# A two-layer Mish block on one core: x tiles 2-3 by a plain load and TensorE transposes instead of the DMA transpose, and ScalarE's first load behind a memset

## The chip, the core and the metric

One core of a Trainium2 chip. Its engines are TensorE (matmuls, accumulating into the 8 banks of PSUM), VectorE, ScalarE, GpSimd and SyncE. Data moves between device memory and the on-chip SBUF by 16 DMA engines; a transfer is issued by SyncE or ScalarE here, each with a queue of its own, and raises a semaphore when it has landed. The metric is the time of the program on the device in microseconds. Lower is better.

## The reference

x is 2048 rows of 512, w1 is 512 x 1792, w2 is 1792 x 512, all bf16.

```python
h = jnp.einsum("bsd,df->bsf", x, w1) + b1
sp = jnp.log1p(jnp.exp(-jnp.abs(h))) + jnp.where(h > 0, h, jnp.zeros_like(h))
act = h * jnp.tanh(sp)                      # Mish
return jnp.einsum("bsf,fd->bsd", act, w2)
```

## The kernel before

The rows of x are taken in four blocks of 512 (four tiles j of 128 rows each). For a block the first projection computes h transposed: for each of 14 column tiles f of w1, four matmuls (the k tiles of the contracted 512) accumulate a 128 x 512 piece in one PSUM bank. ScalarE adds the bias and applies Mish in one instruction into a_sb (L170). Then the second projection takes each of the four row tiles: 14 matmuls over f accumulate 128 x 512 outputs, VectorE copies them to o_sb (L181) and SyncE stores them. So a stage is 56 matmuls of the first projection (L164), then 56 of the second (L193), four times over. The order on every engine is the order in which the code is written; each engine waits on semaphores where the code says so.

The first projection needs x transposed (xT: 512 features over partitions). Blocks 1 to 3 get it from a DMA transpose issued by SyncE (`load_xT`). Block 0 is split so that TensorE can start early: x tiles 0-1 come by a plain load in which each partition takes two consecutive rows of x (2 KB), into x_nat; TensorE transposes them in eight 128 x 128 pieces (`transpose_x`, L145, by the identity matrix that GpSimd builds), into PSUM banks 6, 5 and 4, and VectorE copies them to xT (L149). Because each partition takes rows 2p and 2p+1, the columns of xT are the even rows and then the odd rows, and the stores of output tiles 0 and 1 put the rows back by the same pattern. Tiles 2-3 come by a DMA transpose.

Ahead of that, TensorE runs ten dummy matmuls (L133) on a constant. Behind the transposes stand, in this order: 16 matmuls of 256 columns over x tiles 0-1 (k by k, f 0 to 3 within each k), 16 of 256 columns over x tiles 2-3 (f by f, k 0 to 3 within each f), which complete the first four banks, then f 4 to 7 at 512 columns, and the rest.

Weights: w1 for f 0-3 comes in two pieces on ScalarE's queue (k 0-1, then k 2-3, `FIRST`), and behind them b1. On SyncE's queue stand x_nat, the DMA transpose of tiles 2-3, w1 for f 4-7 in two pieces, w1 for f 8-13, w2 in two pieces, and the DMA transposes of blocks 1 to 3. The bias is turned into a column per f by VectorE: a memset of b1_pad (L122), a copy, four 32 x 32 transposes and a cast (L204 to L209); ScalarE's first Mish waits for that.

Of the kernel before, what the change touches and what calls it, by code (L numbers as in the profile page):

```python
# [5 lines left out]
P = 128  # L6
# [26 lines left out]
def bass_standalone__dense_activation_mish__prompt_kernel(  # L33
# [10 lines left out]
    BF, F32 = dt.bfloat16, dt.float32  # L44

    _, S, D = x.shape
    F = w1.shape[1]
    KT, FT = D // P, F // P
    assert (S, D, F) == (2048, 512, 1792) and sum(BLOCKS) == S
    x2, out2 = x[0], out[0]  # L50
# [3 lines left out]
    F0 = 4  # L54

    with ExitStack() as es:
        def sb(name, shape, t):
            return es.enter_context(nc.sbuf_tensor(name, shape, t))

        x_nat = sb("x_nat", [P, 2, D], BF)  # L60
        xT = sb("xT", [P, KT, S], BF)
        w1_sb = sb("w1_sb", [P, KT, F], BF)
        w2_sb = sb("w2_sb", [P, FT, D], BF)
# [1 line left out]
        b1_pad = sb("b1_pad", [32, P], BF)  # L65
# [3 lines left out]
        ident = sb("ident", [P, P], BF)  # L69
# [4 lines left out]
        def sem(name):  # L74
            return es.enter_context(nc.semaphore(name))

        sp = Stream(nc.sync, None)
        pe = Stream(nc.tensor, sem("c_pe"))
        dve = Stream(nc.vector, sem("c_dve"))
        act = Stream(nc.scalar, sem("c_act"))  # L80
        pool = Stream(nc.gpsimd, sem("c_pool"))

        def load(q, dst, src, name, transpose=False):
            s = sem(name)
            (q.eng.dma_start_transpose if transpose else q.eng.dma_start)(dst, src).then_inc(s, 16)  # L85
            return (s, 16)

        t_w1, t_w2, t_xT = {}, {}, {}

        def load_w1(q, ks, a, b):  # L90
            t = load(q, w1_sb[:, ks, a * P:b * P], w1v[:, ks, a * P:b * P], "s_w1_%d_%d" % (ks.start, a))
            for f in range(a, b):
                for k in range(ks.start, ks.stop):
                    t_w1[k, f] = t
# [6 lines left out]
        def load_xT(lo, hi):  # L101
            t = load(sp, xT[:, :, lo:hi], x2[lo:hi, :], "s_xT%d" % lo, True)
            for j in range(lo // P, hi // P):
                t_xT[j] = t

        for ks in FIRST:
            load_w1(act, slice(*ks), 0, F0)

        x01 = x2[0:2 * P, :].rearrange("(p j) d -> p j d", j=2)
        out01 = out2[0:2 * P, :].rearrange("(p j) d -> p j d", j=2)  # L110
        t_xn = load(sp, x_nat[:, :, :], x01, "s_xn")
        t_b1 = load(act, b1_nat[:, :], b1.rearrange("(j p) -> j p", p=P), "s_b1")
        load_xT(2 * P, 4 * P)
        load_w1(sp, slice(0, 2), 4, 8)
        load_w1(sp, slice(2, KT), 4, 8)
        load_w1(sp, slice(0, KT), 8, FT)
# [2 lines left out]
        for s in range(1, len(BLOCKS)):  # L119
            load_xT(starts[s], starts[s + 1])  # L120

        t_bz = dve.mark(nc.vector.memset(b1_pad[:, :], 0.0))  # L122
        t_ones = pool.mark(pool.eng.memset(ones[:, :], 1.0))  # L123
        pool.wait(t_ones)
        t_id = pool.mark(pool.eng.affine_select(ident[:, :], ones[:, :], pattern=[[1, P]], compare_op=ALU.is_equal,  # L125
                                                fill=0.0, base=0, channel_multiplier=-1))
# [5 lines left out]
        def dummy(n):  # L132
            nc.tensor.matmul(ps[:, 7, 0:n], c_w, c_m[:, 0:n], start=True, stop=True)  # L133

        free = [[] for _ in range(8)]
        t_cp = {}
        t_mish = {}


        def transpose_x(bank, ks):  # L140
            pe.wait(t_xn, t_id, *free[bank])
            psb = ps[:, bank, :].bitcast(BF)
            for i, k in enumerate(ks):
                for j in range(2):
                    mm = nc.tensor.transpose(psb[:, (2 * i + j) * P:(2 * i + j + 1) * P],  # L145
                                             x_nat[:, j, k * P:(k + 1) * P], ident[:, :])
            n = len(ks)
            dve.wait(pe.mark(mm))
            t = dve.mark(nc.vector.tensor_copy(xT[:, ks[0]:ks[0] + n, 0:2 * P],  # L149
                                               psb[:, 0:2 * n * P].rearrange("p (k t) -> p k t", k=n)))  # L150
            for k in ks:
                t_cp[k] = t
            free[bank] = [t]

        def mm1_step(s, f, k, bank, j0=0, j1=None):
            j1 = BLOCKS[s] // P if j1 is None else j1
            lo, hi = j0 * P, j1 * P
            first = k == 0 and j0 == 0
            if first:
                pe.wait(*free[bank])  # L160
            pe.wait(t_w1[k, f])
            for j in range(starts[s] // P + j0, starts[s] // P + j1):
                pe.wait(t_cp[k] if j < 2 else t_xT[j])
            return nc.tensor.matmul(ps[:, bank, lo:hi], w1_sb[:, k, f * P:(f + 1) * P],  # L164
                                    xT[:, k, starts[s] + lo:starts[s] + hi], start=first,
                                    stop=(k == KT - 1 and hi == BLOCKS[s]))
# [11 lines left out]
        def put(i, lo, hi, bank, t_mm, q):  # L178
            nonlocal n_out
            dve.wait(t_mm)  # L180
            t = dve.mark(nc.vector.tensor_copy(o_sb[:, i, lo:hi], ps[:, bank, 0:hi - lo]))  # L181
            free[bank] = [t]
            q.wait(t)
            dst = out01[:, i, lo:hi] if i < 2 else out2[i * P:(i + 1) * P, lo:hi]
            q.eng.dma_start(dst, o_sb[:, i, lo:hi]).then_inc(s_out, 16)
            n_out += 1

        def mm2(i, lo, hi, bank, q=sp):
            s = max(b for b in range(len(BLOCKS)) if starts[b] <= i * P)
            pe.wait(*free[bank])  # L190
            for f in range(FT):
                pe.wait(t_w2[f], t_mish[s, f])
                mm = nc.tensor.matmul(ps[:, bank, 0:hi - lo], a_sb[:, f, i * P:(i + 1) * P], w2_sb[:, f, lo:hi],  # L193
                                      start=(f == 0), stop=(f == FT - 1))
            put(i, lo, hi, bank, pe.mark(mm), q)


        for n in WARM:
            dummy(n)
        transpose_x(6, (0,))  # L200
        transpose_x(5, (1,))
        transpose_x(4, (2, 3))
        dve.wait(t_b1, t_bz)
        t_b1p = dve.mark(nc.vector.tensor_copy(b1_pad[0:FT, :], b1_nat[:, :]))  # L204
        dve.wait(t_b1p)
# [1 line left out]
            t_b1t = dve.mark(nc.vector.transpose(b1_t[c * 32:(c + 1) * 32, :], b1_pad[:, c * 32:(c + 1) * 32]))  # L207
        dve.wait(t_b1t)
        t_b1c = dve.mark(nc.vector.tensor_copy(b1_sb[:, :], b1_t[:, 0:FT]))  # L209
        for k in range(KT):  # L210
            for f in range(F0):
                mm1_step(0, f, k, f, 0, 2)
        for f in range(F0):
            for k in range(KT):
                mm = mm1_step(0, f, k, f, 2, 4)
            mish(0, f, f, pe.mark(mm))
        for f in range(F0, 2 * F0):
            for k in range(2):
                mm1_step(0, f, k, f)
# [5 lines left out]
        for s in range(len(BLOCKS)):  # L225
            for f in range(2 * F0 if s == 0 else 0, FT):
                bank = f % 8 if s == 0 else 4 + f % 4
# [38 lines left out]
```

## Time and profile before

| what | value |
|---|---|
| median of 3 runs | 105.2 us (104.94 to 105.24) |
| profiled execution, own time | 105.35 us |
| its span | 104.1 us |
| TensorE matmuls: busy, share, count | 100.6 us, 97%, 496 |
| ScalarE busy, VectorE busy | 39.0 us, 13.3 us |
| DMA | 7.94 MB in 13361 packets, 7852 of them under 512 B |
| granted TensorE clock | 1.00 throughout |

PE is TensorE's matmuls and PEld its weight loads, DVE is VectorE, ACT ScalarE, SP SyncE; a q behind the name means the engine's instruction queue, where DMAs are issued. A row of a timeline gives the start, the length, the engine, the line, the operation, out<-in with shapes, the count of merged instructions, and in brackets the idle time before with what ended it. w_sb stands for both weight tensors, b_nat and b_pad for the bias buffers. The chain of waits is followed back from the last instruction.

### The profile page before, as it was taken

How to read it: one execution, taken by the hardware profiler on the slowest of the kernel's cores; microseconds unless marked ns; L12 is line 12 of the kernel's file. 1: busy time of each engine (PE TensorE's matmuls, PEld its weight loads, DVE VectorE, ACT ScalarE, POOL GpSimd, SP SyncE). 2: the span in 40 equal slices, each digit the busy share in tenths (PEclk: the TensorE clock that was granted, in tenths of full speed). 3: DMA queues.
4: the chain of work that ended last, by engine and by line, in shares of the span. 5: the costliest groups of instructions: out<-in, count | busy, mean ns of one | idle time of the engine just before them, and what ended most of it. 6: DMA issues, size and time to landing. Idle time of an engine off the chain costs nothing.

```text
span 104.1 us, 1135 instructions
## 1 busy us (share of the span) xinstructions
PE 100.6 (97%) x496; PEld 47.7 (46%) x496; DVE 13.3 (13%) x27; ACT 39.0 (37%) x57; POOL 0.7 (1%) x6
## 2 busy tenths in 40 slices
PE   6889999999999999999999999999999999999992
PEld 2566444444444444444444444444444444444461
DVE  0330000012220000022220000022112000021223
ACT  0408797000027777200007777500005777700000
POOL 2000000000000000000000000000000000000000
DMA  2999999991101000010111000001111000001111
GB/s 47 300 280 368 349 332 197 207 196 50 50 1 50 0 0 0 6 50 8 43 50 50 0 0 0 3 6 50 50 50 50 0 0 0 0 0 57 50 50 50
DMA packets 13361, 7.94 MB, mean 76 GB/s; under 512 B 7852, under 2 KB 13228, under 8 KB 13356
## 3 DMA queue, kind: packets, MB, share of 16 engines
q1 hardware_dynamic: 12640, 7.31, 26.5%
q10 hardware_dynamic: 716, 0.56, 1.7%
q8 instruction: 4, 0.07, 0.3%
q14 instruction: 1, 0.01, 0.0%
HBM read 3.94 MB, written 2.10 MB: 58 GB/s over the span
## 4 chain that ended last, share of the span: by engine, by line
PE 92%; DMA 5%; ACTq 0%; DVE 0%; issue 0%
PE ps L193 46%; PE ps L164 46%; DMA w_sb<-in_w_dram 5%; ACTq L85 0%; DVE o_sb L181 0%
## 5 line engine op out<-in xcount | busy, mean ns | idle before, releaser
L170 ACT ACTIVATE a_sb<-ps,b_sb 128x512 bf16<-128x512 f32 x56 | 37.7, 688 | 49.2 <-PE ps L164 45.0
L164 PE MATMUL ps<-xT,w_sb 128*128 128x512 bf16 (+1 forms) x240 | 49.3, 365 | 0.5 <-DMA w_sb<-in_w_dram 0.4
L193 PE MATMUL ps<-w_sb,a_sb 128*128 128x512 bf16 (+2 forms) x238 | 49.0, 366 | 0.0
L164 PEld LDWEIGHTS ps<-xT,w_sb 128*128 128x128 bf16 x240 | 23.2, 98 | 25.8 <-DMA w_sb<-in_w_dram 1.0
L193 PEld LDWEIGHTS ps<-w_sb,a_sb 128*128 128x128 bf16 x238 | 22.8, 98 | 25.9
L181 DVE CAST o_sb<-ps 128x512 bf16<-128x512 f32 (+2 forms) x17 | 11.2, 660 | 83.2 <-PE ps L193 83.2
L133 PE MATMUL ps<-const-bfloat16-1.0 128*128 128x512 bf16 (+1 forms) x10 | 2.8, 464 | 0.8 <-PEq L251 0.8
L127 ACT ACT_TABLE_LOAD x1 | 1.3, 1283 | 2.5 <-issue 2.5
L133 PEld LDWEIGHTS ps<-const-bfloat16-1.0 128*128 128x128 bf16 x10 | 1.2, 139 | 2.2 <-issue 2.2
L149 DVE COPY xT<-ps 128x256 bf16<-128x256 bf16 (+1 forms) x3 | 0.8, 329 | 3.2 <-PE ps L145 3.2
L207 DVE STREAM_TRANSPOSE b_t<-b_pad 32x32 bf16<-32x32 bf16 x4 | 0.8, 202 | 0.1
L145 PE MATMUL ps<-ident,x_nat 128*128 128x128 bf16 x8 | 0.6, 220 | 0.2 <-DMA x_nat<-in_x_dram 0.2
L145 PEld LDWEIGHTS ps<-ident,x_nat 128*128 128x128 bf16 x8 | 0.5, 98 | 0.4 <-DMA x_nat<-in_x_dram 0.4
L204 DVE COPY b_pad<-b_nat 14x128 bf16<-14x128 bf16 x1 | 0.2, 183 | 1.8 <-DMA b_nat<-in_b_dram 1.8
L125 POOL TENSOR_SCALAR_AFFINE_SELECT ident<-ones 128x128 bf16<-128x128 bf16 x1 | 0.3, 292 | 0.1
L122 DVE MEMSET b_pad<- 32x64 uint32 x1 | 0.1, 112 | 0.9 <-PEq L251 0.9
L123 POOL MEMSET ones<- 128x128 bf16 x1 | 0.2, 204 | 0.3 <-POOLq L251 0.3
L209 DVE CAST b_sb<-b_t 128x14 f32<-128x14 bf16 x1 | 0.2, 176 | 0.0
L251 POOL MEMSET const-bfloat16-1.0<- 128x1 bf16 x1 | 0.1, 101 | 0.0
L251 POOL MEMSET const-uint8-127<- 128x1 uint8 x1 | 0.1, 101 | 0.0
L251 POOL MEMSET const-float32-0.0<- 128x1 f32 x1 | 0.1, 98 | 0.3 <-issue 0.3
L251 POOL MEMSET const-float32-1.0<- 128x1 f32 x1 | 0.1, 98 | 0.0
## 6 DMA issues: line engine op xcount, KB each, us to landing
out_dram<-o_sb SPq DMA_DIRECT2D x15, 128.0 KB, 1.7
w_sb<-in_w_dram SPq DMA_DIRECT2D x1, 1152.0 KB, 10.4
w_sb<-in_w_dram SPq DMA_DIRECT2D x1, 768.0 KB, 6.7
w_sb<-in_w_dram SPq DMA_DIRECT2D x1, 640.0 KB, 8.0
w_sb<-in_w_dram ACTq DMA_DIRECT2D x2, 256.0 KB, 4.2
w_sb<-in_w_dram SPq DMA_DIRECT2D x2, 256.0 KB, 5.0
x_nat<-in_x_dram SPq DMA_DIRECT2D x1, 256.0 KB, 3.0
out_dram<-o_sb SPq DMA_DIRECT2D x1, 96.0 KB, 1.6
```

The costliest lines, as they stand in the source:

```text
L123: t_ones = pool.mark(pool.eng.memset(ones[:, :], 1.0))
L125: t_id = pool.mark(pool.eng.affine_select(ident[:, :], ones[:, :], pattern=[[1, P]], compare_op=ALU.is_equal, fill=0.0, base=0, channel_mu ...
L127: act.eng.preload_act_table(ACT.Mish)
L133: nc.tensor.matmul(ps[:, 7, 0:n], c_w, c_m[:, 0:n], start=True, stop=True)
L145: mm = nc.tensor.transpose(psb[:, (2 * i + j) * P:(2 * i + j + 1) * P], x_nat[:, j, k * P:(k + 1) * P], ident[:, :])
L149: t = dve.mark(nc.vector.tensor_copy(xT[:, ks[0]:ks[0] + n, 0:2 * P], psb[:, 0:2 * n * P].rearrange("p (k t) -> p k t", k=n)))
L164: return nc.tensor.matmul(ps[:, bank, lo:hi], w1_sb[:, k, f * P:(f + 1) * P], xT[:, k, starts[s] + lo:starts[s] + hi], start=first, stop=( ...
L170: t = act.mark(act.eng.activation(a_sb[:, f, starts[s]:starts[s + 1]], ps[:, bank, 0:BLOCKS[s]], ACT.Mish, bias=b1_sb[:, f:f + 1]))
L181: t = dve.mark(nc.vector.tensor_copy(o_sb[:, i, lo:hi], ps[:, bank, 0:hi - lo]))
L193: mm = nc.tensor.matmul(ps[:, bank, 0:hi - lo], a_sb[:, f, i * P:(i + 1) * P], w2_sb[:, f, lo:hi], start=(f == 0), stop=(f == FT - 1))
L207: t_b1t = dve.mark(nc.vector.transpose(b1_t[c * 32:(c + 1) * 32, :], b1_pad[:, c * 32:(c + 1) * 32]))
L251: nc = _bacc.Bacc("TRN2", target_bir_lowering=False, num_devices=1)
```

## The change

x_nat grows to two pairs of tiles. A helper, `pair`, gives the view of two tiles in which partition p holds rows 2p and 2p+1. SyncE loads x tiles 0-1 and then tiles 2-3 by it; the DMA transpose of tiles 2-3 is gone. `transpose_x` takes the pair b. The second pair is transposed by eight more TensorE transposes in two groups of four, into banks 6 and 5, placed between the 256-column matmuls of k 1 and those of k 2; VectorE copies each group to xT. The bias work on VectorE now stands behind these copies in the code. Output tiles 2 and 3 are stored by the `pair` view as tiles 0 and 1 are. The memset of b1_pad stands first, and ScalarE waits for it before it issues its first load of w1.

```diff
-        x_nat = sb("x_nat", [P, 2, D], BF)
+        x_nat = sb("x_nat", [P, 4, D], BF)
...
+        def pair(t, b):
+            return t[2 * b * P:2 * (b + 1) * P, :].rearrange("(p j) d -> p j d", j=2)
+
+        t_bz = dve.mark(nc.vector.memset(b1_pad[:, :], 0.0))
+        act.wait(t_bz)
         for ks in FIRST:
             load_w1(act, slice(*ks), 0, F0)
-
-        x01 = x2[0:2 * P, :].rearrange("(p j) d -> p j d", j=2)
-        out01 = out2[0:2 * P, :].rearrange("(p j) d -> p j d", j=2)
-        t_xn = load(sp, x_nat[:, :, :], x01, "s_xn")
+        t_xn = [load(sp, x_nat[:, 2 * b:2 * b + 2, :], pair(x2, b), "s_xn%d" % b) for b in range(2)]
         t_b1 = load(act, b1_nat[:, :], b1.rearrange("(j p) -> j p", p=P), "s_b1")
-        load_xT(2 * P, 4 * P)
         load_w1(sp, slice(0, 2), 4, 8)
...
-        t_bz = dve.mark(nc.vector.memset(b1_pad[:, :], 0.0))
...
-        def transpose_x(bank, ks):
-            pe.wait(t_xn, t_id, *free[bank])
+        def transpose_x(b, bank, ks):
+            pe.wait(t_xn[b], t_id, *free[bank])
...
-                                             x_nat[:, j, k * P:(k + 1) * P], ident[:, :])
+                                             x_nat[:, 2 * b + j, k * P:(k + 1) * P], ident[:, :])
...
-            t = dve.mark(nc.vector.tensor_copy(xT[:, ks[0]:ks[0] + n, 0:2 * P],
+            t = dve.mark(nc.vector.tensor_copy(xT[:, ks[0]:ks[0] + n, 2 * b * P:2 * (b + 1) * P],
...
-                pe.wait(t_cp[k] if j < 2 else t_xT[j])
+                pe.wait(t_cp[j // 2, k] if j < 4 else t_xT[j])
...
-            dst = out01[:, i, lo:hi] if i < 2 else out2[i * P:(i + 1) * P, lo:hi]
+            dst = pair(out2, i // 2)[:, i % 2, lo:hi] if i < 4 else out2[i * P:(i + 1) * P, lo:hi]
...
-        transpose_x(6, (0,))
-        transpose_x(5, (1,))
-        transpose_x(4, (2, 3))
+        transpose_x(0, 6, (0,))
+        transpose_x(0, 5, (1,))
+        transpose_x(0, 4, (2, 3))
+        for k in range(KT):
+            if k == 2:
+                transpose_x(1, 6, (0, 1))
+                transpose_x(1, 5, (2, 3))
+            for f in range(F0):
+                mm1_step(0, f, k, f, 0, 2)
         dve.wait(t_b1, t_bz)
...
-        for k in range(KT):
-            for f in range(F0):
-                mm1_step(0, f, k, f, 0, 2)
```

How this moves instructions is seen at two places. On TensorE, from the first transposes to the first matmuls of 512 columns. The semaphores are named for what they count: c_dve VectorE's steps, s_xn the load of x_nat (s_xn0 and s_xn1 after), s_w1_k_f the piece of w1 that begins at k and f, s_xT256 the DMA transpose of tiles 2-3. Before:

```order
L145 MATMUL ps<-ident,x_nat 128x128 [waits c_pool,s_xn]
L145 MATMUL ps<-ident,x_nat 128x128 x7
L164 MATMUL ps<-xT,w_sb 128x256 [waits c_dve,s_w1_0_0]
L164 MATMUL ps<-xT,w_sb 128x256 x3
L164 MATMUL ps<-xT,w_sb 128x256 [waits c_dve]
L164 MATMUL ps<-xT,w_sb 128x256 x3
L164 MATMUL ps<-xT,w_sb 128x256 [waits c_dve,s_w1_2_0]
L164 MATMUL ps<-xT,w_sb 128x256 x7
L164 MATMUL ps<-xT,w_sb 128x256 [waits s_xT256]
L164 MATMUL ps<-xT,w_sb 128x256 x15
L164 MATMUL ps<-xT,w_sb 128x512 [waits s_w1_0_4]
```

And in the change:

```order
L165 MATMUL ps<-xT,w_sb 128x256 [waits c_dve,s_w1_0_0]
L165 MATMUL ps<-xT,w_sb 128x256 x3
L165 MATMUL ps<-xT,w_sb 128x256 [waits c_dve]
L165 MATMUL ps<-xT,w_sb 128x256 x3
L146 MATMUL ps<-ident,x_nat 128x128 [waits s_xn1]
L146 MATMUL ps<-ident,x_nat 128x128 x7
L165 MATMUL ps<-xT,w_sb 128x256 [waits c_dve,s_w1_2_0]
L165 MATMUL ps<-xT,w_sb 128x256 x7
L165 MATMUL ps<-xT,w_sb 128x256 [waits c_dve]
L165 MATMUL ps<-xT,w_sb 128x256
L165 MATMUL ps<-xT,w_sb 128x256 [waits c_dve]
L165 MATMUL ps<-xT,w_sb 128x256 x13
```

Eight transposes stand between the eight matmuls of k 0-1 and those of k 2-3, with a wait for the second x load, and the wait for the DMA transpose has become two waits for VectorE's copies.

The other place is the head of SyncE's queue. Before and then after:

```order
L85 DMA x_nat<-in_x_dram 128x1024 [waits barrier_Pool_Activation_PE_DVE_SP_release]
L85 DMA_TRANSPOSE xT<-in_x_dram 128x4x256
L85 DMA w_sb<-in_w_dram 128x2x512 x2
L85 DMA w_sb<-in_w_dram 128x4x768
L85 DMA w_sb<-in_w_dram 128x5x512
```

```order
L85 DMA x_nat<-in_x_dram 128x1024 [waits barrier_Pool_Activation_PE_DVE_SP_release]
L85 DMA x_nat<-in_x_dram 128x1024
L85 DMA w_sb<-in_w_dram 128x2x512 x2
L85 DMA w_sb<-in_w_dram 128x4x768
L85 DMA w_sb<-in_w_dram 128x5x512
```

The second place in the queue is a plain load now; the rest is as it was. On ScalarE the first row, `L85 DMA w_sb<-in_w_dram 128x2x512`, waits for c_dve beside the barrier, and its order is unchanged.

More of the change, by code (lines that the diff above doesn't have):

```diff
@@ L145, in transpose_x @@
                     mm = nc.tensor.transpose(psb[:, (2 * i + j) * P:(2 * i + j + 1) * P],
-                                             x_nat[:, j, k * P:(k + 1) * P], ident[:, :])
+                                             x_nat[:, 2 * b + j, k * P:(k + 1) * P], ident[:, :])
             n = len(ks)
             dve.wait(pe.mark(mm))
-            t = dve.mark(nc.vector.tensor_copy(xT[:, ks[0]:ks[0] + n, 0:2 * P],
+            t = dve.mark(nc.vector.tensor_copy(xT[:, ks[0]:ks[0] + n, 2 * b * P:2 * (b + 1) * P],
                                                psb[:, 0:2 * n * P].rearrange("p (k t) -> p k t", k=n)))
             for k in ks:
-                t_cp[k] = t
+                t_cp[b, k] = t
             free[bank] = [t]
```

## The prediction

> **What bounds the kernel now.** I read the page's shares first, then the chain of waits, then the timeline of the first ten microseconds, and last the DMA issues in narrow windows, because the first three lead there.
>
> From the page of the kernel before:
>
> ```profile
> span 104.1 us, 1135 instructions
> ```
>
> From its chain in order of time (start, length, what):
>
> ```profile
> 1.29 4.70 DMA w_sb<-in_w_dram
> 5.98 0.05 issue
> 6.03 11.52 PE ps L164 x64
> 17.55 12.09 PE ps L193 x56
> ...
> 90.07 12.14 PE ps L193 x70
> ```
>
> TensorE works without a hole from 6.03 us to the end: each later stage of 56 matmuls takes the same 12.09 us. The change touches nothing there. What can move is when that unbroken run begins, and how much first-projection work is already done by then. The timeline of the start shows it (start, length, engine, line, count, idle before and its releaser):
>
> ```profile
> 0.80 0.98 ACTq L85 DMA_DIRECT2D w_sb<-in_w_dram  x2
> 0.81 0.40 SPq L85 DMA_DIRECT2D x_nat<-in_x_dram  x1
> 0.84 2.81 PE L133 MATMUL ps<-const-bfloat16-1.0 128*128 128x512 bf16 x10 [0.84 <-PEq L251]
> 0.87 0.11 DVE L122 MEMSET b_pad<- 32x64 uint32 x1 [0.87 <-PEq L251]
> ...
> 1.26 1.31 SPq L85 DMA_TRANSPOSE xT<-in_x_dram  x1
> ...
> 2.62 3.53 SPq L85 DMA_DIRECT2D w_sb<-in_w_dram  x5
> ...
> 3.83 0.62 PE L145 MATMUL ps<-ident,x_nat 128*128 128x128 bf16 x8 [0.19 <-DMA x_nat<-in_x_dram]
> 4.16 0.82 DVE L149 COPY xT<-ps 128x256 bf16<-128x256 bf16 x3 [3.17 <-PE ps L145]
> 4.56 0.78 PEld L164 LDWEIGHTS ps<-xT,w_sb 128*128 128x128 bf16 x8 [0.28 <-DMA w_sb<-in_w_dram]
> 4.59 1.03 PE L164 MATMUL ps<-xT,w_sb 128*128 128x256 bf16 x8
> 6.03 0.77 PEld L164 LDWEIGHTS ps<-xT,w_sb 128*128 128x128 bf16 x8 [0.68 <-DMA w_sb<-in_w_dram]
> 6.03 11.52 PE L164 MATMUL ps<-xT,w_sb 128*128 128x256 bf16 x64 [0.41 <-DMA w_sb<-in_w_dram]
> ...
> 6.99 10.06 PEld L164 LDWEIGHTS ps<-xT,w_sb 128*128 128x128 bf16 x56 [0.20 <-DMA xT<-in_x_dram]
> ```
>
> And the two shapes whose rate I need, from the groups by line with shapes apart:
>
> ```profile
> L164 PE MATMUL ps<-xT,w_sb 128*128 128x256 bf16 x32 | 3.9, 273 | 0.5 <-DMA w_sb<-in_w_dram 0.4
> L145 PE MATMUL ps<-ident,x_nat 128*128 128x128 bf16 x8 | 0.6, 220 | 0.2 <-DMA x_nat<-in_x_dram 0.2
> L149 DVE COPY xT<-ps 128x256 bf16<-128x256 bf16 x2 | 0.5, 286 | 3.2 <-PE ps L145 3.2
> L149 DVE COPY xT<-ps 128x512 bf16<-128x512 bf16 x1 | 0.4, 415 | 0.0
> ```
>
> Matmuls overlap, so their mean of 273 or 220 ns is no price. The price is the step from one start to the next: (1.03 - 0.27) / 7 = 0.109 us for a 256-column matmul, (0.62 - 0.22) / 7 = 0.057 us for a transpose. With these the holes behind 4.59 can be sized. Eight matmuls (k 0 and 1) are through at 4.59 + 8 x 0.109 = 5.46; the ninth starts at 6.03, when the second ScalarE piece of w1 (k 2 and 3) has landed: **a hole of 0.57 us**. Eight more end at 6.03 + 0.87 = 6.90; the next weights load starts at 6.99, released by the DMA transpose of x tiles 2-3: **a hole of 0.09 us**. Nothing else is lost after 4.59.
>
> What sets 4.59 itself? x_nat and the first w1 piece, and then a short chain: transposes at 3.83, the first copy from 4.16 to 4.45 (0.286 us each). Issues in the window 0.7 to 1.1 (KB, us to landing):
>
> ```profile
> w_sb<-in_w_dram ACTq DMA_DIRECT2D x1, 256.0 KB, 3.6
> x_nat<-in_x_dram SPq DMA_DIRECT2D x1, 256.0 KB, 3.0
> ```
>
> x_nat lands at 0.81 + 3.0 = 3.8, the first w1 piece at 0.80 + 3.6 = 4.4. So w1 and the copied x are ready within 0.1 us of each other, and the first real matmul starts 0.1 us later. The timeline names the DMA, but the copy is as late: a gain at only one of them buys nothing.
>
> **The change part by part.** The reckoning is against the profiled execution: span 104.10 us, its own time 105.35, so 1.25 us lie around the span. The median shown is 105.20, 0.15 under that execution; I carry a difference of spans over to the median.
>
> *Eight transposes added.* They stand in TensorE's order between k 1 and k 2, exactly in the 0.57 us hole: 8 x 0.057 = 0.46 us. If x tiles 2-3 are there by 5.46, they run from 5.46 to 5.92. If they found no hole they would cost those 0.46 us in full.
>
> *The wait for the DMA transpose removed.* The 0.09 us hole at 6.99 goes. In its place the matmuls of columns 256-511 wait for two copies of four transposes each. Such a copy, 128x512, took 0.415 us. The first four transposes are out at about 5.46 + 4 x 0.057 + 0.16 (the 220 ns latency beyond a step) = 5.85, the copies run to 6.27 and 6.69. They are wanted at 5.92 + 8 x 0.109 = 6.79 and, for k 2, two matmuls later at 7.01. Cover 0.3 to 0.5 us, so nothing. The bias work on VectorE is queued behind these copies; it began only at
>
> ```profile
> 6.74 0.18 DVE L204 COPY b_pad<-b_nat 14x128 bf16<-14x128 bf16 x1 [1.76 <-DMA b_nat<-in_b_dram]
> ```
>
> so 6.69 does not delay it, and ScalarE's activations have slack after it (their first stage is not in the chain).
>
> *The hole before k 2.* It shrinks to whatever is left if the second w1 piece lands after 5.92. It landed at 1.29 + 4.7 = 5.99 while the DMA transpose was in flight. These are the DMA views of four stretches (1.8 to 2.8, 2.8 to 3.4, 3.4 to 4.0, 5.0 to 5.6 us); q1 is SyncE's queue, q10 ScalarE's, as their byte totals show:
>
> ```profile
> q1 hardware_dynamic: 90, 0.18, 85.2%
> ```
> ```profile
> q10 hardware_dynamic: 129, 0.13, 63.0%
> q1 hardware_dynamic: 52, 0.08, 36.6%
> ```
> ```profile
> q10 hardware_dynamic: 221, 0.21, 110.8%
> q1 hardware_dynamic: 4, 0.00, 0.6%
> ```
> ```profile
> DMA packets 242, 0.07 MB, mean 110 GB/s; under 512 B 236, under 2 KB 242, under 8 KB 242
> q1 hardware_dynamic: 234, 0.06, 105.7%
> q10 hardware_dynamic: 8, 0.01, 3.1%
> ```
>
> First x_nat alone, then w1 alone, with a short overlap: the pieces went through nearly one after the other, at about 350 GB/s. Then the small packets of the DMA transpose fill the engines at 110 GB/s while the last eight packets of w1 trickle out. With 2 KB rows in place of these, 256 KB take 0.26 MB / 350 GB/s = 0.75 us. If x tiles 0-1, w1 k 0-1, x tiles 2-3 and w1 k 2-3 pass in this order, the last lands about two pieces (1.5 us, at best 1.2 by the 0.6 us that lay between the landings of x_nat and w1) after the first w1 piece: 4.4 + 1.2 to 1.5 = 5.6 to 5.9. Just in time; the x piece lands near 5.1, in time for 5.46. I take no hole.
>
> *The start, 4.59.* Two edits act on it. ScalarE now waits for the memset, which ends at 0.87 + 0.11 = 0.98, so w1 is issued near 1.04 instead of 0.80: 0.24 later. And x tiles 2-3 are issued behind x tiles 0-1 on SyncE at 1.26, in a form that goes out at once. If the first w1 piece is queued behind x_nat anyway, as the first two stretches above suggest, the 0.24 us cost nothing: its data moved only from 2.8 on. Lower bound: x_nat, alone at the start, lands earlier; the dummy matmuls ahead of the transposes end at 0.84 + 2.81 = 3.65, with some 0.2 us of latency in that, so TensorE is free near 3.46, at most 0.37 us before 3.83. Upper bound: the whole of x tiles 2-3 goes ahead of w1, +0.6 to +0.75 us. I take 0, the order of the trace.
>
> *The rest.* SyncE's issue of a DMA transpose took 1.31 us against 0.40 for a plain load, so the later weight loads go out about 0.9 us earlier. They were not late: w1 for f 4-7 went out at 2.62 and landed 4.9 later (below), for a use at 6.99 + 16 x 0.109 = 8.73. It is a gain on no path. Output tiles 2-3 are written as alternate 1 KB rows, as tiles 0-1 were already; they are issued long before the end. Nothing.
>
> ```profile
> w_sb<-in_w_dram SPq DMA_DIRECT2D x1, 256.0 KB, 4.9
> ```
>
> **Sum:** -0.57 - 0.09 + 0.46 + 0 = -0.20 us. Span 103.90, time 105.00.
>
> **The rivals.**
>
> 1. *x arrives earlier.* [...] For it: in the stretch 1.8 to 2.8 x_nat moved only 184 GB/s in the trace, so its start has room. Against it: w1 must come earlier too, and it can do so only by following a shorter x_nat. About 0.25 us (two thirds of the 0.37 bound): 104.75.
>
> 2. *The third piece gets ahead of the first w1 piece* (the other side). w1 issued 0.24 later, x tiles 2-3 already on SyncE's queue: if the engines take them first, w1 k 0-1 lands at 5.0 to 5.15, and TensorE, whose order puts the new transposes behind k 1, has nothing else to do. Start 4.59 + 0.6 = 5.19, less the 0.20: +0.40, 105.60; half shared, +0.10, 105.30. It decides from 0.20 us of delay on. For it: SyncE issues x tiles 2-3 only 0.22 us after w1, and a plain load needs less time on the queue. Against it: w1's first data came the moment x_nat was through, so w1 was waiting there. [...]
>
> 3. *The wait for w1 k 2-3 remains.* SyncE's next loads now go out at about 1.7 instead of 2.62, and may share the engines with it. If it still lands at 5.99, only 5.92 to 6.03 is lost: 105.10. A landing at 6.3 would cost 0.4: 105.4.
>
> 4. *The transposes don't run at 0.057.* If each took its full 0.22 us, 1.76 us would stand in place of 0.46: 106.3. The eight of the trace exclude it as far as they go: they took 0.62 together. [...]
>
> **How the numbers follow.** Forecast 0.45, rival 1 0.25, rival 2 0.18, rival 3 0.10, rival 4 0.02. The time is the forecast's, 105.00; its own range is 104.8 to 105.2. The range for all reaches to 104.6 (most of rival 1) and 105.55 (all of rival 3, most of rival 2). A measurement of this kernel can tell about 0.3%, 0.32 us, so faster means under 104.88 and slower over 105.52. Faster: a fifth of the forecast's chance and nearly all of rival 1: 0.33. Slower: rivals 4 and most of 2: 0.15. Same: 0.52.
>
> **What would show it.** In the changed kernel's timeline: the new eight transposes should start within 0.05 us of the end of the first eight 256-column matmuls, and the matmuls of k 2 right behind them with no wait for w1. The first 256-column matmul at 4.55 to 4.65 is the forecast; at 4.3 to 4.4 rival 1; at 4.9 or later rival 2, with a landing of ScalarE's first load more than 3.6 us after its issue. A wait for w_sb behind the second transposes is rival 3. The forecast is wrong if the 512-column stage begins anywhere but near 8.54 (8.73 before).

## The result, and the profile after

| | before | after |
|---|---|---|
| median of 8 runs each | 105.1 us (104.78 to 105.34) | 105.86 us (105.32 to 106.39) |
| ratio, 95% interval | | 1.0063 [1.0039, 1.0087] |
| profiled span | 104.1 us | 104.6 us |
| second projection of block 0 begins | 17.55 us | 18.00 us |
| first 512-column matmul | 8.75 us | 9.20 us |

The forecast was 105.0, 0.20 us faster; the change made the kernel slower, by 0.76 us between the medians and 0.66 us by the ratio, whose interval leaves out 1. The page and the chain of the changed kernel (start, length, what):

```profile
span 104.6 us, 1153 instructions
```
```profile
4.64 0.44 DVE xT L150
5.08 0.04 issue
5.12 1.05 PE ps L165 x8
6.17 0.45 PE ps L146 x8
6.61 11.38 PE ps L165 x64
18.00 12.09 PE ps L194 x56
```

As before, TensorE runs without a hole behind the start and each later stage still takes 12.09 us, so the loss of 0.45 us of span lies wholly ahead of 9.20. The timeline of the changed kernel there:

```profile
3.57 1.04 PE L146 MATMUL ps<-ident,x_nat 128*128 128x128 bf16 x8
...
5.12 0.77 PEld L165 LDWEIGHTS ps<-xT,w_sb 128*128 128x128 bf16 x8 [0.78 <-DMA w_sb<-in_w_dram]
5.12 1.05 PE L165 MATMUL ps<-xT,w_sb 128*128 128x256 bf16 x8 [0.52 <-DVE xT L150]
...
6.00 0.61 PE L146 MATMUL ps<-ident,x_nat 128*128 128x128 bf16 x8
6.43 0.75 DVE L150 COPY xT<-ps 128x512 bf16<-128x512 bf16 x2 [1.36 <-PE ps L146]
...
6.57 4.74 PE L165 MATMUL ps<-xT,w_sb 128*128 128x256 bf16 x33
```

In this profile x_nat came earlier: its transposes start at 3.57 instead of 3.83. But the first real matmul starts at 5.12 instead of 4.59. The chain names VectorE's copy as the releaser, since the third copy ended last; the first matmul needs only the first copy, which ended some 0.8 us before that (4.00 + 0.29). What it waited for is in the row of the weight loads: w1. The issues of the changed kernel one by one (the windows 1.21 to 1.24, 1.44 to 1.45 and 1.70 to 1.71; they were issued at 1.01, 1.25 and 1.46):

```profile
w_sb<-in_w_dram ACTq DMA_DIRECT2D x1, 256.0 KB, 4.1
```
```profile
x_nat<-in_x_dram SPq DMA_DIRECT2D x1, 256.0 KB, 4.5
```
```profile
w_sb<-in_w_dram ACTq DMA_DIRECT2D x1, 256.0 KB, 5.1
```

So w1 k 0-1 landed at 5.1 (4.4 before), x tiles 2-3 at 5.8, w1 k 2-3 at 6.5 (6.0 before). The eight new transposes sit without a gap behind the first eight matmuls, as planned, and the next matmul follows at 6.57 instead of 6.46: the second w1 piece is again the last to come.

### The profile page after: what moved, and what is told of

It reads as the page before. It is cut to its first block, busy times and chain, and to the rows that moved or that the text cites. A ratio compares the mean times of both kernels' runs of the same rounds, so it can differ in the third digit from the quotient of the medians.

```text
span 104.6 us, 1153 instructions
## 1 busy us (share of the span) xinstructions
PE 101.3 (97%) x504; PEld 48.6 (46%) x504; DVE 14.2 (14%) x29; ACT 39.0 (37%) x57; POOL 0.7 (1%) x6
## 4 chain that ended last, share of the span: by engine, by line
PE 97%; DVE 1%; issue 0%
PE ps L165 47%; PE ps L194 46%; PE ps L134 3%; PE ps L146 1%; DVE xT L150 0%; DVE o_sb L182 0%
## 5 line engine op out<-in xcount | busy, mean ns | idle before, releaser
L150 DVE COPY xT<-ps 128x512 bf16<-128x512 bf16 (+1 forms) x5 | 1.7, 368 | 4.5 <-PE ps L146 4.4
L146 PE MATMUL ps<-ident,x_nat 128*128 128x128 bf16 x16 | 1.6, 265 | 0.0
L146 PEld LDWEIGHTS ps<-ident,x_nat 128*128 128x128 bf16 x16 | 1.3, 120 | 0.2 <-DMA x_nat<-in_x_dram 0.2
```

The source lines that it names most:

```text
L150: t = dve.mark(nc.vector.tensor_copy(xT[:, ks[0]:ks[0] + n, 2 * b * P:2 * (b + 1) * P], psb[:, 0:2 * n * P].rearrange("p (k t) -> p k t", ...
```

## The experiments

Two theories at first. **W**: ScalarE's wait makes both w1 pieces late. **C**, later sharpened to **Q**: the two queues take turns at the DMA engines, whole loads at a time, and a plain load second on SyncE's queue now takes the turn between the two w1 pieces, which the DMA transpose had come too late to take.

### The two edits apart

Without ScalarE's wait, all else as changed:

```diff
-        act.wait(t_bz)
```

> The changed kernel without ScalarE's wait for the memset; all else as changed. Theory W (the wait: w1 issued 0.21 us later misses its place on the DMA engines): the first w1 piece lands near 4.4 again instead of 5.07, the first 256-column matmul starts near 4.6 instead of 5.12, the 512-column stage near 8.6 instead of 9.20, time 105.0 to 105.2. Theory C (the second plain x load competes with w1, whoever issues first): the w1 landing stays at 4.9 or later and the time at 105.6 to 105.9.

105.55 us (12 runs), ratio to the kernel before 1.0037 [1.0004, 1.0069]. w1 k 0-1 landed at 4.7, between the two expectations, and w1 k 2-3 at 6.4, as late as with the wait. Its TensorE rows:

```profile
4.76 1.82 PE L164 MATMUL ps<-xT,w_sb 128*128 128x256 bf16 x8 [0.19 <-DMA w_sb<-in_w_dram]
6.42 0.61 PE L145 MATMUL ps<-ident,x_nat 128*128 128x128 bf16 x8
```

So the wait isn't what loses the time, or not most of it: the intervals with and without it overlap, and the second w1 piece is as late. A second thing shows: eight 256-column matmuls took 1.82 us here, not 1.05, a step of 0.21 us. TensorE ran at half rate until about 6.4; the last section returns to that.

The kernel before with the wait alone:

```diff
+        t_bz = dve.mark(nc.vector.memset(b1_pad[:, :], 0.0))
+        act.wait(t_bz)
         for ks in FIRST:
             load_w1(act, slice(*ks), 0, F0)
...
-        t_bz = dve.mark(nc.vector.memset(b1_pad[:, :], 0.0))
```

> The kernel before with only ScalarE's wait for the memset added; the DMA transpose of tiles 2-3 stays. W: the first w1 piece lands near 5.0, the first 256-column matmul starts near 5.1, the second w1 piece lands after 6.3, time 0.4 to 0.6 us over the kernel before. C: w1 lands by 4.65, time within 0.2 us of the kernel before.

Neither expectation held. One execution took 105.77 us and five 108.95 to 111.11, so no ratio is given and no price of the wait follows; the profile is of the longest and tells of that execution alone. Its TensorE rows, its issues at 1.70 to 1.75, and its windows (us, busy times by engine, granted TensorE clock, DMA share, GB/s):

```profile
5.55 1.05 PE L165 MATMUL ps<-xT,w_sb 128*128 128x256 bf16 x8 [0.85 <-DMA w_sb<-in_w_dram]
9.14 1.25 PE L165 MATMUL ps<-xT,w_sb 128*128 128x256 bf16 x5 [2.54 <-DMA w_sb<-in_w_dram]
```
```profile
w_sb<-in_w_dram ACTq DMA_DIRECT2D x1, 256.0 KB, 7.6
xT<-in_x_dram SPq DMA_TRANSPOSE x1, 7.8
```
```profile
9.00:12.00 3.00, 2.86 (x14) 2.01 (x15) 1.17 (x6) 0.02 (x1) 0.00 (x0) 0.50 1.08 366
12.00:14.00 2.00, 2.00 (x11) 1.36 (x10) 0.00 (x0) 1.73 (x3) 0.00 (x0) 0.50 1.11 350
```

With w1 issued 0.21 us later, the second w1 piece and the DMA transpose land together at 9.1. The DMA queues of this execution between 3.9 and 4.5 us, and of another profile of the kernel before in the same stretch (packets, MB, and the packets' times added up as a share of 16 engines, which passes 100% where they overlap):

```profile
q1 hardware_dynamic: 411, 0.11, 187.8%
q10 hardware_dynamic: 16, 0.01, 29.8%
```
```profile
q10 hardware_dynamic: 184, 0.18, 87.3%
q1 hardware_dynamic: 105, 0.03, 26.7%
```

In the kernel before ScalarE's w1 has the engines then; here the transpose's small packets do, ahead of w1 k 2-3. In the long hole that follows, the granted TensorE clock went from 1.00 (6.6 to 7.9 us) to 0.50 (8 to 9 us). In this execution, then, the late issue of w1 cost much together with the DMA transpose; that the other long executions went the same way is not shown. The changed kernel has no DMA transpose there.

### Who is second on each queue

In the changed kernel, the second x load issued by ScalarE, behind both w1 pieces (the wait kept); and then, without the wait, by ScalarE between them. In both, w1 for f 4-7 becomes second on SyncE's queue.

```diff
-        t_xn = [load(sp, x_nat[:, 2 * b:2 * b + 2, :], pair(x2, b), "s_xn%d" % b) for b in range(2)]
+        t_xn = [load(q, x_nat[:, 2 * b:2 * b + 2, :], pair(x2, b), "s_xn%d" % b) for b, q in enumerate((sp, act))]
```

> The changed kernel with the second x load issued by ScalarE behind both w1 pieces instead of by SyncE; the wait is kept. SyncE's next load, w1 for f 4-7, takes its place in SyncE's queue. W: the first w1 piece still lands near 5.0. C, if it is the second x load as such: w1 lands near 4.4 to 4.6, x tiles 2-3 near 6.0, and the start moves to 4.65. If it is any plain load second on SyncE's queue, w1 stays near 5.0 as by W, and the x tiles come late: over 106.

> The changed kernel without the wait, and the second x load issued by ScalarE between the two w1 pieces. On one queue w1 k 0-1 cannot be overtaken by it. W and C: w1 lands near 4.4, x tiles 2-3 near 5.1, the second w1 piece near 5.8, first matmul 4.6, the 512-column stage near 8.55, time 104.9 (0.2 under the kernel before). If SyncE's w1 for f 4-7, now second on its queue, competes as the x load did, w1 lands later than 4.8 and the time is 105.4 or more.

107.61 us, ratio 1.0241 [1.0182, 1.03], and 107.19 us, ratio 1.0188 [1.015, 1.0226]: far over: the first as it was expected for any plain load second on SyncE's queue, the second against the 104.9 that W and C gave. But w1 k 0-1 landed at 4.2 and 4.4. The first of the two, issue by issue (windows 1.21 to 1.24, 1.45 to 1.46, 1.70 to 1.71, 2.05 to 2.10; issued at 1.01, 1.25, 1.47, then 1.72 and 2.00):

```profile
w_sb<-in_w_dram ACTq DMA_DIRECT2D x1, 256.0 KB, 3.2
```
```profile
w_sb<-in_w_dram SPq DMA_DIRECT2D x1, 256.0 KB, 3.7
```
```profile
w_sb<-in_w_dram ACTq DMA_DIRECT2D x1, 256.0 KB, 4.3
```
```profile
w_sb<-in_w_dram SPq DMA_DIRECT2D x1, 256.0 KB, 5.4
x_nat<-in_x_dram ACTq DMA_DIRECT2D x1, 256.0 KB, 5.5
```

Landings at 4.2 (ScalarE), 5.0 (SyncE), 5.8 (ScalarE), 7.1 (SyncE), 7.5 (ScalarE), after x_nat (SyncE) at 3.5: the queues alternate, a load each, about 0.75 us apiece for the first ones. The second x load, third on ScalarE's queue, came sixth in all, and TensorE stood waiting for it. In the second kernel, where ScalarE's loads landed in their order on the queue (w1 k 0-1 at 4.4, x tiles 2-3 at 6.0), it was w1 k 2-3 that came sixth, at 7.9. This is Q's picture, and it takes W away: with the wait kept, w1 k 0-1 landed as early as anywhere.

### The turn taken away, and how steady the landings are

SyncE waits until x_nat has landed before it issues the second x load, so that this load can't have the turn between the w1 pieces; then the same without ScalarE's wait and with the transposes between k 2 and k 3.

```diff
-        t_xn = [load(sp, x_nat[:, 2 * b:2 * b + 2, :], pair(x2, b), "s_xn%d" % b) for b in range(2)]
+        t_xn = [load(sp, x_nat[:, 0:2, :], pair(x2, 0), "s_xn0")]
+        sp.wait(t_xn[0])
+        t_xn.append(load(sp, x_nat[:, 2:4, :], pair(x2, 1), "s_xn1"))
```

> The changed kernel, only that SyncE waits for x_nat to land before it issues the load of x tiles 2-3, so that this load cannot take the turn between the two w1 pieces; ScalarE's wait is kept. Theory Q (turns): the first w1 piece lands at 4.2 to 4.4, the second by 5.3, 0.6 or more sooner than in the changed kernel; x tiles 2-3 only near 5.9, so the time doesn't fall: the transposes wait and the 512-column stage begins near 9.0. Rival D (ScalarE's late issue delays both w1 pieces): the second w1 piece stays at 5.9 or later.

> As the run ahead of it, but without ScalarE's wait and with the eight transposes between k 2 and k 3, where x tiles 2-3 should just have landed. Q: second w1 piece by 5.3, transposes at 5.9, 512-column stage near 8.65, time 0.2 to 0.3 us over the kernel before, level with or just under the changed kernel. If transposes and their copies cost nothing at the start, it would equal the kernel before.

106.2 us, ratio 1.0111 [1.0081, 1.014], and 106.06 us, ratio 1.0091 [1.006, 1.0122]. The issues of the first at 1.21 to 1.30, 1.50 to 1.60 and 3.70 to 3.80 (issued at 1.01, 1.47 and 3.65):

```profile
w_sb<-in_w_dram ACTq DMA_DIRECT2D x1, 256.0 KB, 3.3
```
```profile
w_sb<-in_w_dram ACTq DMA_DIRECT2D x1, 256.0 KB, 3.6
```
```profile
x_nat<-in_x_dram SPq DMA_DIRECT2D x1, 256.0 KB, 2.8
```

Now w1 lands at 4.3 and 5.1, 0.7 apart, with ScalarE's wait in place: the 5.9 to 6.5 of the changed kernel was the x load's turn. (SyncE's later loads are held back here too; that a load of w1 in that place took the turn too is seen in the first run of the section before, where w1 for f 4-7 stood there and landed at 5.0, and w1 k 2-3 at 5.8.) The rival that blamed the late issue falls. The price is the x load itself at 6.4, later than the 5.9 expected, and the second kernel was slower than foreseen (half rate until 6.7 in its profile). Neither is a way out.

The changed kernel timed once more beside these, and two more profiles each of the two kernels:

> The changed kernel, timed beside the next three on one chip. As before: 0.3 to 0.6% over the kernel before, second w1 piece at 5.9 to 6.6.

> The kernel before, unchanged, profiled again: are its landings steady? Theory Q (turns of the two queues decide: with the DMA transpose late, both w1 pieces follow x_nat directly; with a plain load second on SyncE's queue they take turns with it): the second w1 piece lands by 6.0, as in the first profile (5.98). Theory N (the landings of single profiles are chance): it lies anywhere from 5.4 to 6.6, overlapping the changed kernel's.

> As the run ahead of it: Q: second w1 piece by 6.0; N: anywhere from 5.4 to 6.6.

> The changed kernel, unchanged, profiled again. Q: order of landing x_nat, w1 k 0-1, x tiles 2-3, w1 k 2-3, each 0.6 to 0.8 us behind the other, the last at 5.9 to 6.6, and the 512-column stage begins 2.6 to 2.7 us behind it or, where the TensorE clock is raised late, behind the half-rate matmuls. N: another order in some profile, the second w1 piece down to 5.4.

> As the run ahead of it: Q: the same order, second w1 piece at 5.9 to 6.6; N: another order.

Timed again: 105.51 us, ratio 1.0043 [1.0012, 1.0074]. Landings of the two w1 pieces, read from the issue rows:

| profile | w1 k 0-1 | w1 k 2-3 | first 512-column matmul | span |
|---|---|---|---|---|
| before, first | 4.4 | 6.0 | 8.75 | 104.1 |
| before, second and third | 4.3, 4.2 | 5.3, 5.5 | 8.39, 8.36 | 103.7, 103.7 |
| after, first | 5.1 | 6.5 | 9.20 | 104.6 |
| after, second and third | 4.6, 4.5 | 6.0, 5.9 | 8.70, 8.61 | 104.1, 104.0 |
| after, timed again | 4.6 | 6.0 | 9.07 | 104.4 |

The second w1 piece spreads by some 0.6 us in either kernel. Q's order holds in all seven, and the middle of the changed kernel's landings is 0.5 us later (6.0 against 5.5). The two ranges just overlap (5.9 against 6.0), so these seven alone don't rule out theory N. Of the kernels below whose loads are the same, two with the loads of before landed it at 5.5 and 5.2 (eight transposes more; no dummies), and the changed kernel without dummies at 6.0, each near its own kind. The profile that the forecast was read from is the slow end of the kernel before: its hole before k 2 was 0.57 us, against 0.32 here (third profile of the kernel before, TensorE rows):

```profile
4.36 1.03 PE L164 MATMUL ps<-xT,w_sb 128*128 128x256 bf16 x8
5.54 0.77 PEld L164 LDWEIGHTS ps<-xT,w_sb 128*128 128x128 bf16 x8 [0.44 <-DMA w_sb<-in_w_dram]
5.55 4.48 PE L164 MATMUL ps<-xT,w_sb 128*128 128x256 bf16 x31 [0.16 <-DMA w_sb<-in_w_dram]
...
6.59 3.16 PEld L164 LDWEIGHTS ps<-xT,w_sb 128*128 128x128 bf16 x24 [0.28 <-DMA xT<-in_x_dram]
```

And the third profile of the changed kernel:

```profile
4.55 1.05 PE L165 MATMUL ps<-xT,w_sb 128*128 128x256 bf16 x8 [0.26 <-DMA w_sb<-in_w_dram]
5.32 0.54 PEld L146 LDWEIGHTS ps<-ident,x_nat 128*128 128x128 bf16 x8
5.43 0.61 PE L146 MATMUL ps<-ident,x_nat 128*128 128x128 bf16 x8
5.85 0.76 DVE L150 COPY xT<-ps 128x512 bf16<-128x512 bf16 x2 [1.05 <-PE ps L146]
5.98 3.81 PEld L165 LDWEIGHTS ps<-xT,w_sb 128*128 128x128 bf16 x31
5.98 4.09 PE L165 MATMUL ps<-xT,w_sb 128*128 128x256 bf16 x30
```

This pair closes: the start 0.19 later, transposes 0.46, a hole of 5.98 - 5.43 - 0.46 = 0.09 before k 2; away go the holes of 5.55 - 4.36 - 0.87 = 0.32 and 6.59 - 5.55 - 0.87 = 0.17. Together +0.25, and the first 512-column matmul moved by 8.61 - 8.36 = 0.25 too.

### The price of the transposes alone

The kernel before with eight more transposes of x_nat at the same place, results unused, its loads untouched:

```diff
         for k in range(KT):
+            if k == 2:
+                pe.wait(*free[6], *free[5])
+                for n in range(8):
+                    nc.tensor.transpose(ps[:, 6 - n // 4, :].bitcast(BF)[:, (n % 4) * P:(n % 4 + 1) * P],
+                                        x_nat[:, n % 2, (n // 2) * P:(n // 2 + 1) * P], ident[:, :])
```

> The kernel before with eight extra transposes of x_nat, whose results nobody reads, between k 1 and k 2; its loads are untouched. It prices the transposes without any change of transfers. Theory Q (the transfers set the start, the transposes fill holes): within 0.15 us of the kernel before, the 512-column stage within 0.1 of 8.37 to 8.75. Theory P (TensorE's 0.46 us of transposes is the loss): 0.3 to 0.5 us over the kernel before.

105.34 us (12 runs), ratio 1.0019 [0.9989, 1.0049]; first 512-column matmul at 8.49.

```profile
4.48 1.03 PE L164 MATMUL ps<-xT,w_sb 128*128 128x256 bf16 x8
5.24 0.54 PEld L214 LDWEIGHTS ps<-ident,x_nat 128*128 128x128 bf16 x8
5.35 0.61 PE L214 MATMUL ps<-ident,x_nat 128*128 128x128 bf16 x8
...
5.80 4.37 PE L164 MATMUL ps<-xT,w_sb 128*128 128x256 bf16 x31
...
6.73 3.16 PEld L164 LDWEIGHTS ps<-xT,w_sb 128*128 128x128 bf16 x24 [0.18 <-DMA xT<-in_x_dram]
```

The transposes fill the hole before k 2, as the forecast had it, and the wait for the DMA transpose still ends last. At this place, then, TensorE's 0.46 us alone are no loss: the medians are level (105.34 against 105.33). The interval reaches to 0.5 us and doesn't exclude theory P by itself; the rows do, for this execution.

### Two terms that stayed open

Is it the 2 KB rows of the second x load that make the first w1 piece late? The second pair loaded with 1 KB rows (partition p takes rows p and p+128 of the pair), twice:

```diff
-            return t[2 * b * P:2 * (b + 1) * P, :].rearrange("(p j) d -> p j d", j=2)
+            return t[2 * b * P:2 * (b + 1) * P, :].rearrange(("(p j) d -> p j d", "(j p) d -> p j d")[b], j=2)
```

> The changed kernel with x tiles 2-3 loaded as two rows of 1 KB per partition (rows p and p+128) instead of one run of 2 KB; output tiles 2-3 stored to match. Theory R (2 KB rows hold up the w1 piece ahead of them): first w1 piece lands at 4.2 to 4.45. Theory S (any x load there does): 4.5 or later. The turns are the same by both: second w1 piece 0.6 to 0.8 us behind x tiles 2-3.

> The same kernel as the run ahead of it, profiled a second time. R: first w1 piece at 4.2 to 4.45; S: 4.5 or later.

w1 k 0-1 landed at 4.4 and 4.5 (issued at 1.01, 3.4 and 3.5 to landing), one on either side; w1 k 2-3 at 5.9 and 6.1, the same turns. With 4.5 to 5.1 in the changed kernel it is not settled by the landings; the rate at which w1 came, below, says that the 2 KB rows are at least not needed.

And does the half-rate stretch cost the changed kernel more? Both kernels without the ten dummy matmuls:

```diff
-WARM = (512,) * 5 + (128,) * 5
+WARM = ()
```

> The kernel before without the ten dummy matmuls, so that TensorE's first work is the transposes and its clock is raised late. Theory K (late clock): 256-column matmuls step by 0.213 us up to at least 7 us; 1 to 2.5 us over the kernel before.

> The changed kernel without the dummies. Theory K: the eight added transposes now take 0.85 us at half rate and no hole takes them up, so the gap to the run ahead of it is 0.6 to 1.0 us, more than the 0.3 to 0.75 us with dummies. If the clock has no part in the loss, the gap stays at 0.3 to 0.5 us.

106.23 us, ratio 1.0122 [1.0086, 1.0158], and 106.78 us, ratio 1.0174 [1.0135, 1.0213]. The ratios to the same kernel differ by 0.0052, 0.55 us: just under what K said, and within what two kernels with dummies differ by. In the single profiles the first 512-column matmul came at 9.42 and 10.21, 0.79 apart, and the added transposes took 1.06 us instead of 0.61. The table of seven profiles holds a closer comparison. The changed kernel's second profile and the timed one have the same landings (4.6 and 6.0), but the first 512-column matmul came at 8.70 and 9.07. In the timed one the first eight 256-column matmuls took 1.56 us instead of 1.05, so most of them ran at half rate:

```profile
4.61 1.56 PE L165 MATMUL ps<-xT,w_sb 128*128 128x256 bf16 x8
```

In the second profile of the kernel before, half rate up to about 5.3 us (the first four took 0.98 us) cost next to nothing, 8.39 against 8.36: there was a hole to take it up. So a late change to the full rate cost the changed kernel 0.37 us in one profile; how often it does so, and what it makes of the median, is not shown.

No version that was run beats the kernel before. By the rows above there was little to win: without any hole the changed kernel would need 4.36 + 32 x 0.109 + 0.46 = 8.31 to the first 512-column matmul, against 8.36 to 8.39.

## Why the prediction was wrong

**Where the kernel is bound**: right. Nothing behind the first 512-column matmul moved, and the start is set by landings.

**Transposes, copies, bias**: right. Eight in 0.61 us, without a gap behind k 1; the copies cost nothing; the DMA transpose's hole went. With the loads untouched the transposes cost nothing at the median. Rival 4 (0.22 us each) is out.

**The start, "I take 0, the order of the trace"**: this is the main step that failed. It measured +0.53 us in the first pair of profiles, +0.11 and +0.19 in the second and third. As a point in time the forecast's 4.59 was nearly met, 4.55 to 4.63 in three of four profiles; but the kernel before starts at 4.36 and 4.52 in its other two, so against it the term is not 0. The order of landing was as forecast: x_nat, w1 k 0-1, x tiles 2-3, w1 k 2-3, in every profile. So rival 2 in its full form, the x load ahead of w1, did not come, although its sign was the result's. But in that order the first w1 piece still came later than behind a DMA transpose. The windows 3.2 to 3.6 us, before and then after, show the engines part idle while it was due (369 against 136 GB/s; 382 against 215 in the second profile of each):

```profile
3.20:3.60 0.40, 0.40 (x5) 0.20 (x2) 0.00 (x0) 0.40 (x1) 0.00 (x0) 1.00 1.05 369
```
```profile
3.20:3.60 0.40, 0.40 (x6) 0.23 (x4) 0.00 (x0) 0.40 (x1) 0.00 (x0) 1.00 0.63 136
```

In that window the changed kernel moves rows of w1 alone. The x load then begins before the w1 piece is through: by 3.8 us 147 of its 256 rows had moved, and between 3.8 and 4.6 both queues are at work (the queues of the changed kernel's first profile, 3.2 to 3.6 and 3.8 to 4.6):

```profile
q10 hardware_dynamic: 53, 0.05, 62.5%
```
```profile
q1 hardware_dynamic: 94, 0.18, 59.3%
q10 hardware_dynamic: 130, 0.12, 44.6%
```

So rival 2's half-shared form was nearer the truth in this profile than "queued behind x_nat anyway". Whether the two moved on the same engines the views don't tell.

The wait isn't the cause: 4.71 without it, and 4.2 and 4.4 with it once the second x load was gone from its place. The drop in rate goes with the queue. From 2.8 to 3.6 us the engines moved 347 to 375 GB/s in all eight profiles in which SyncE's second transfer is a DMA transpose or is held back by a wait, and 198 to 316 in all ten in which it is a plain load, x in 2 KB rows, x in 1 KB rows (253 and 316) or w1 (315 and 284) alike. Why the rate was lower while a load waited on the other queue is open, and so is why the first w1 piece came late with x there and hardly with w1 there.

Rival 1's gain is not shown. In the first pair x_nat's transposes began 0.26 us earlier, but x_nat landed at 3.8, 3.6 and 3.5 us in the kernel before and at 3.5 to 3.6 in the changed one. Where it did come earlier it bought nothing, since w1 did not come earlier with it: the condition that the forecast itself had named against it.

**The second w1 piece, "4.4 + 1.2 to 1.5"**: the spacing was right (0.7 + 0.7 in the first profile), its foot was not: 5.1 in place of 4.4, or 4.5 to 4.6 in the others, so it landed at 5.9 to 6.5 and left a hole of about 0.1 us. What I missed is what this turn costs next to the kernel before, in which w1 k 2-3 followed k 0-1 directly and landed at 5.3 to 5.5 in two of three profiles. I took 5.99, one profile's value, for the kernel's. This is the second step that failed.

**The sum against one profile**: the holes to be filled were 0.66 us in that execution and 0.49 in the third profile. With the third profile's holes the forecast's own sum gives 0.46 - 0.49 = -0.03 even with the start at 0: no change, not a gain. This was readable beforehand only in part: the profiled 105.35 lay above all three times shown.

What is left: taken in order, the first three profiles of the two kernels differ by 0.25 to 0.45 us at the first 512-column matmul, the two timings by 0.66 and 0.45 by their ratios (0.76 and 0.18 between the medians). The rest, some 0.2 us, is not accounted for. A late change to the full rate acts that way, 0.37 us in the one pair of profiles with equal landings, but its share is not shown.

## What to carry to other kernels

The load that was made quicker to issue here (0.42 us on SyncE's queue against the DMA transpose's 1.31) also took its turn sooner: it landed at 5.8 us, between the two w1 pieces, where the DMA transpose had landed at 7.0, behind both. Before replacing a slow transfer, list in order what both queues hold, let plain loads alternate load by load as they did here (4.2, 5.0, 5.8 us in one run), and see which landing is pushed back by one turn: here w1 k 2-3. And size holes of less than a microsecond from several profiles of the same kernel; one profile's hole before k 2 was 0.57 us where another's was 0.32.

## What the runs showed of the hardware

**The two queues alternated by whole loads, as their landings show it.** Landings in one run: 3.5, 4.2, 5.0, 5.8, 7.1, 7.5 us for SyncE, ScalarE, SyncE, ScalarE, SyncE, ScalarE. The turns are not strict: between 3.8 and 4.6 us in the changed kernel both queues moved rows, 94 packets of SyncE's and 130 of ScalarE's. How single engines took them the views don't tell.

**While a plain load waited second on SyncE's queue, the engines moved less.** 198 to 316 GB/s from 2.8 to 3.6 us in ten profiles with one, 347 to 375 in eight without.

**TensorE came to its full rate at a different time from execution to execution, and in one execution the granted clock fell.** The step of a 256-column matmul was 0.109 us or 0.21 us. The column of the granted clock reads 1.00 in the slow stretches at the start too, so the step has to be read; the "1.00 throughout" of the table before the change is that column. The rate had changed from slow to fast before the transposes at 3.83 in the first profile of the kernel before (eight in 0.62 us), and not before 6.7 in the run with the transposes between k 2 and k 3 (twelve 256-column matmuls took 2.50 us from 4.53 on), with the same ten dummies. In the run with the wait alone, TensorE had no work from 6.6 to 9.1 us. The granted clock was 1.00 from 6.6 to 7.9, 0.50 from 8 to 9, still inside the hole, and 0.50 in the windows 9 to 12 and 12 to 14, quoted above; the 24 256-column matmuls from 9.14 on took 5.30 us, 0.22 each. That the slow stretches at the start, with nearly the same step, are the clock's too is an estimate from these two steps; the column does not show it. A start-up change of a few tenths is measured through them.
